# Picking the next expert tiles on GpSimd with one MAX8, and two small operations moved to GpSimd

## The chip, the cores and the metric

The kernel runs on one core of a Trainium2 chip. The metric is the time of one execution on the device in microseconds; the time shown is the median of three runs. Engines: TensorE (PE, with PEld for its weight loads), VectorE (DVE), ScalarE (ACT), GpSimd (POOL) and SyncE (SP), which here only issues DMAs.

## The reference

```python
# attention: q, k, v of 8 batches x 8 heads x 576 x 64
scores = scale * np.matmul(q, k.transpose(0, 1, 3, 2))
kth = np.partition(scores, -32, axis=-1)[..., -32:-31]
scores = np.where(scores >= kth, scores, -1e9)
attn = softmax(scores)                # exp, and the sum with 1e-9 added
x = np.matmul(attn, v)                # to 4608 rows of 512
# experts: 8, of 512 x 1024 x 512; each row goes to one
logits = x @ w_gate
e_idx = np.argmax(logits, axis=1)
gate_w = softmax(logits)[chosen]
eom = 1.0 / (1.0 + np.exp(-(x @ w_output_gate)))
out[mask] = gate_w * eom[:, e] * (np.maximum(x[mask] @ w1[e], 0.0) @ w2[e])
```

## The kernel before

**Attention steps.** The 4608 rows are 36 tiles of 128 queries. A step does two heads (an even and an odd one) of one tile, so a tile takes four steps and there are 144; four more rounds of the loop drain what is behind. In a step VectorE finds the largest of each group of scores (L305), ranks them (L312, L315) and, one step later, takes the largest of what lies below the 24th (L354) and chooses the 32nd (L365, `choose`). ScalarE copies the scores from PSUM (L286, called s), makes a sign against the 24th for each head (L339) and the exponentials (L349); GpSimd adds sign and scores (L342, two operations of 128x576) and copies two columns for a later check (L371, `near`). VectorE then multiplies the exponentials with the mask and sums them (`weigh`, L381). TensorE transposes the weights and multiplies with v.

**Lone heads.** In the first `LONE` steps the odd head isn't weighed on VectorE: `choose` writes the negated 32nd score to `LESS`, ScalarE makes a second sign with it (`veil`, L388), GpSimd adds sign and scores (L391), and two steps later ScalarE takes the exponential and the sum in one (`unveil`, L397). The steps that are below `LONE` are called calm: they have an order of their own, with the scores two steps ahead and with transposes of a constant that keep TensorE at work in every other step.

**Rows.** When a tile's four steps are through, `tile_rows` makes `r`, the reciprocal of the sums (an addition of 1e-9 and a reciprocal), computes its logits and writes its rows to memory. Tiles are in groups that end at the tiles listed in `SORTS`. After a group's last tile `group_route` finds the expert of each row, its place among the expert's rows and its weight, and `route` queues one scatter for each tile, which writes the row's index to that place.

**Slots.** A slot is up to 128 rows of one expert. After a group `slot_table` lists the next slots (`EARLY`: how many) from the counts of rows that wait; the last table, after all tiles, lists `USUAL` more, and code behind a condition handles any beyond these. A slot's steps are to load w1 and w2 (2 MB each) of its expert, load the list of rows (`fetch_id`), gather the rows (`fetch_x`), transpose them (`turn_ahead`) and do four pieces of products: two of `up` (L725) and two of `down` (L740). In the steps from `LONE` on, one piece is put into each step. After the last step the rest of the slots run in the tail, in another form: weights, rows and hidden values are split into a high and a low part (L1020, L1021), and three products of parts replace one (L1048).

**Queues.** Small VectorE work waits in `urgent` and `small`, and `fill(n)` issues n of it at fixed places of a step. A member of `small` that returns False stays ahead of the others. GpSimd's slow work (scatters, and the table in pieces of four operations) waits in `slow` with a cost and a due step; `run_slow` issues it up to a budget in each step. Engines work in the order of issue.

Of the kernel before, what the change touches and what calls it, by code (L numbers as in the profile page):

```python
# [33 lines left out]
DMAS = 2.0  # L34
# [5 lines left out]
def tile_topk_attention_moe(  # L40
# [50 lines left out]
    ENDS, EARLY, LEAST = zip(*sorts) if sorts else ((), (), ())  # L91
# [5 lines left out]
    for g in range(NGRP - 1):  # L97
        rest += len(GROUPS[g]) * P
        rest = min(rest, max(E * (LEAST[g] - 1), rest - EARLY[g] * LEAST[g]))
# [19 lines left out]
    first_row = consts.tile([1, E + 1], F32, name="first_row")  # L119
    slot_iota = consts.tile([1, MAXS, E], F32, name="slot_iota")  # L120
# [8 lines left out]
    def setup():  # L129
# [5 lines left out]
        def gates():  # L135
            for a in range(2):
# [12 lines left out]
               iota(first, [[-1, E]], E), iota(carry0, [[REG, E]]),  # L149
# [38 lines left out]
    def run(exact, stack):  # L188
# [170 lines left out]
        def choose(i):  # L359
# [3 lines left out]
            for a in range(2):  # L363
# [82 lines left out]
        done0 = consts.tile([1, E], F32, name="done0")  # L446
        nc.gpsimd.memset(done0, 0.0)
        DONE = [done0]
        rows_done = [0]

        def tile_rows(t, g, lg, j):
# [53 lines left out]
            urgent.append(lambda: nc.vector.tensor_scalar(r, sm, 1e-9, None, op0=ALU.add))  # L505
# [79 lines left out]
        def slot_table(g, last):  # L585

            n = NLAST if last else EARLY[g]
            least = 1 if last else LEAST[g]
            eng = nc.vector if last else nc.gpsimd
# [29 lines left out]
            add(lambda: eng.tensor_tensor(first_row[:, :E], first_row[:, :E], DONE[0], op=ALU.add))  # L619
            if last:  # L620
                def count():
                    NEED.append(consts.tile([1, 1], I32, name="need" + tagged))
                    eng.tensor_copy(NEED[0], T["d"][:, 7 + E:8 + E])
                    if not exact:
                        eng.tensor_scalar(over, T["d"][:, 7 + E:8 + E], -float(usual), 0.0, op0=ALU.add, op1=ALU.max)
# [630 lines left out]
```

## Time and profile before

| what | value |
|---|---|
| time, median of 3 runs | 1275.3 us (1271.2 to 1276.9) |
| the profiled execution's own time | 1271.3 us |
| its span, first to last instruction | 1269.5 us |
| mean granted TensorE clock | 0.99 |
| busy: TensorE, VectorE, ScalarE, GpSimd | 1178.2, 1196.9, 1043.9, 759.0 us |
| slots in all, by loads of w1 | 40 |

The busy times are sums over stages with different limits, so they don't say alone what sets the time. The time of an execution holds the span and what lies before the first and behind the last instruction.

### The profile page before, as it was taken

Reading aid. Unit: us, or ns where it says so; the run is one execution under the profiler, and the core shown is the slowest. Engines: PE = TensorE matmul, PEld = TensorE weight load, DVE = VectorE, ACT = ScalarE, POOL = GpSimd, SP = SyncE. Lnnn points to the kernel's source line nnn. Section 1 sums busy time; section 2 is a strip of 40 time slices with the busy share of each in tenths; the row PEclk is TensorE's granted clock in tenths of the full one; section 3 lists DMA queues with packets and bytes.
Section 4 is the critical chain, followed back from the end, with each engine's and each line's share of the span. In section 5 each row is a group of like instructions: output and inputs, shape, how many; then the busy total and the mean of one; then the engine's idle time right before and its main releaser. Section 6 shows DMA issues by size and latency. Waiting matters only on the chain.

```text
span 1269.5 us, 31280 instructions
## 1 busy us (share of the span) xinstructions
PE 1178.2 (93%) x9792; PEld 896.6 (71%) x9792; DVE 1196.9 (94%) x6157; ACT 1043.9 (82%) x1984; POOL 759.0 (60%) x1222
## 2 busy tenths in 40 slices
PE   6888778777699999999999999999999999999997
PEld 5665556555477777777777777777777777788885
DVE  7999999999999999999999999999999984898984
ACT  6999999898888878888888887888888763798884
POOL 6666666698775766757667667567657753132110
PEclk8999999999899999999999999999999999999999
DMA  5400210202818662765464555765554467999982
GB/s 138 77 18 19 71 55 18 56 19 64 290 57 278 202 225 104 249 229 159 174 205 159 211 189 164 258 221 177 207 179 162 151 202 248 373 399 386 379 311 82
DMA packets 109378, 227.41 MB, mean 179 GB/s; under 512 B 14858, under 2 KB 33546, under 8 KB 108176
## 3 DMA queue, kind: packets, MB, share of 16 engines
q1 hardware_dynamic: 99536, 205.67, 48.4%
q0 software_dynamic: 7552, 18.96, 4.3%
q8 instruction: 79, 1.29, 0.5%
q10 hardware_dynamic: 2112, 0.68, 0.3%
q14 instruction: 99, 0.81, 0.2%
HBM read 206.68 MB, written 20.69 MB: 179 GB/s over the span
## 4 chain that ended last, share of the span: by engine, by line
PE 59%; DVE 26%; issue 10%; DMA 2%; POOL 2%; ACT 1%; POOLq 0%; SPq 0%; ACTq 0%
PE pm L725 14%; PE pm L740 13%; PE po L440 10%; PE ps L278 9%; PE pst L408 9%; DVE cand L305 8%; DVE v L354 5%; DVE cand L315 3%; DVE v L312 3%; DVE ep L381 3%; DMA w1t<-in_w_dram 2%; DVE x L365 1%; PE pm L1048 1%; PE pst L461 1%; POOL xg L704 1%
## 5 line engine op out<-in xcount | busy, mean ns | idle before, releaser
L342 POOL TENSOR_TENSOR w<-s,marks 128x576 f32<-128x576 f32 x288 | 362.8, 1281 | 181.4 <-ACT marks L339 170.8
L305 DVE MAX8 cand<-s 128x8 f32<-128x72 f32 x2304 | 322.0, 218 | 8.1 <-ACT s L286 8.1
L408 PE MATMUL pst<-ident,ep 128*128 128x128 f32 x1296 | 206.8, 284 | 55.9 <-ACT ep L397 48.3
L339 ACT ACTIVATE marks<-s,v 128x576 int8<-128x576 f32 x288 | 220.9, 770 | 34.3 <-DVE v L312 30.8
L408 PEld LDWEIGHTS pst<-ident,ep 128*128 128x128 f32 x1296 | 145.8, 142 | 143.6 <-ACT ep L397 59.4
L416 ACT ACTIVATE pT<-pst 128x512 f32<-128x512 f32 (+1 forms) x432 | 197.7, 481 | 7.0 <-PE pst L408 5.2
L354 DVE MAX8 v<-w 128x8 f32<-128x576 f32 x288 | 202.1, 743 | 0.0
L286 ACT ACTIVATE s<-ps 128x1152 f32<-128x1152 f32 (+1 forms) x145 | 162.3, 1120 | 44.9 <-PE ps L278 44.9
L725 PE MATMUL pm<-xs,w1t 128*128 128x128 f32 x1664 | 194.7, 275 | 0.1
L725 PEld LDWEIGHTS pm<-xs,w1t 128*128 128x128 f32 x1664 | 189.9, 192 | 0.3 <-ACT y L747 0.3
L381 DVE SCALAR_TENSOR_TENSOR ep<-s,kth,ep 128x576 f32<-128x576 f32 x240 | 187.9, 812 | 0.3 <-issue 0.3
L278 PE MATMUL ps<-kst,qst 64*128 64x288 f32 (+1 forms) x1280 | 181.0, 431 | 5.4 <-ACT s L286 5.4
L440 PE MATMUL po<-pT,v 128*64 128x128 f32 (+3 forms) x3200 | 185.3, 267 | 0.0
L440 PEld LDWEIGHTS po<-pT,v 128*64 128x64 f32 (+1 forms) x3200 | 157.9, 136 | 33.0 <-issue 31.3
L740 PE MATMUL pm<-w2t,ht 128*128 128x512 f32 x400 | 180.5, 594 | 0.0
L349 ACT ACTIVATE ep<-s,v 128x576 f32<-128x576 f32 x240 | 175.5, 778 | 0.0
L751 POOL DMA_INDIRECT out_dram<-y,idt x40 | 46.6, 1165 | 181.4 <-ACT y L747 164.5
L312 DVE MAX8 v<-cand 128x8 f32<-128x64 f32 x864 | 148.2, 213 | 0.0
L278 PEld LDWEIGHTS ps<-kst,qst 64*128 64x128 f32 (+1 forms) x1280 | 97.7, 177 | 44.2 <-issue 16.1
L740 PEld LDWEIGHTS pm<-w2t,ht 128*128 128x128 f32 x400 | 72.1, 190 | 71.9 <-issue 71.9
L315 DVE MATCH_REPLACE8 cand<-v,cand 128x64 f32<-128x64 f32 x576 | 116.1, 209 | 0.0
L391 POOL TENSOR_TENSOR w<-s,marks 128x576 f32<-128x576 f32 x48 | 61.5, 1280 | 52.0 <-ACT marks L388 51.9
(183 smaller groups left out, 1837.6 us busy)
## 6 DMA issues: line engine op xcount, KB each, us to landing
w1t<-in_w_dram SPq DMA_DIRECT2D x40, 2048.0 KB, 10.0
w2t<-in_w_dram SPq DMA_DIRECT2D x40, 2048.0 KB, 11.9
v<-in_va_dram SPq DMA_DIRECT2D x8, 1152.0 KB, 5.7
x_rows<-xu SPq DMA_DIRECT2D x36, 256.0 KB, 2.6
qst<-in_qa_dram SPq DMA_DIRECT2D x70, 128.0 KB, 10.8
kst<-in_ka_dram SPq DMA_DIRECT2D x14, 576.0 KB, 7.8
ids<-far SPq DMA_DIRECT2D x1, 678.0 KB
xg<-x_rows,idt POOLq DMA_INDIRECT x40, 6.9
```

What stands on the lines that cost most here:

```text
L278: nc.tensor.matmul(ps[qs, a, n, :288], Q[t][rows, hp, qs], K[b][rows, hp, cols], start=True, stop=True)
L305: nc.vector.max(out=c[:, 8 * g:8 * g + 8], in_=SC[i, a][:, g * GW:(g + 1) * GW])
L312: nc.vector.max(out=vs[:, a, 8 * r:8 * r + 8], in_=cs[a])
L339: nc.scalar.activation(m.bitcast(I8).rearrange("p (s b) -> p s b", b=2)[:, :, 1], s, AF.Sign, bias=vs[:, a, PIVOT - 1:PIVOT], scale=-(1.0 ...
L342: nc.gpsimd.tensor_tensor(w, s, m, op=ALU.add)
L354: nc.vector.max(out=VV[i][0][:, a, 24:32], in_=SW[i][0][a])
L381: nc.vector.scalar_tensor_tensor(e, SC.pop((i, a)), kth_col(i, a), e, op0=ALU.is_ge, op1=ALU.mult, accum_out=SM[t][:, 2 * hp + a:2 * hp + ...
L408: nc.tensor.transpose(ps[:, c - c0, :], pt[:, c * P:(c + 1) * P], ident)
L416: nc.scalar.activation(x, ps[:, :n, :], AF.Copy)
L440: nc.tensor.matmul(po[a * 64:(a + 1) * 64, k, qs], lhs, rhs, start=half and not k and not m, stop=(c == 3 and k == 1 and m == len(TT[t]) - 1))
L725: nc.tensor.matmul(ph[:, f - f0, :], w[:, c, f * P:(f + 1) * P], XS[s][:, c, :], start=(c == 0), stop=(c == NC - 1))
L740: nc.tensor.matmul(PY[s], HT[s][:, f, :], w[:, f, :], start=(f == 0), stop=(f == NF - 1))
```

## The change

The plan `SORTS` has ten groups in place of nine, with 31 early slots in place of 29, and the last table lists 9 in place of 11. The first group, of four tiles, has no slots; the second ends at tile 7 as the first did before. `LONE` falls from 48 to 40. An early table is made by `slot_picks`: a key for each expert (the rows that wait, at most 128, with the expert's number to break ties), one MAX8 on VectorE that sorts the eight keys, and the first n of them; a slot no longer needs a least number of rows, and an expert gets at most one slot in a table. Its other operations run on GpSimd, or on VectorE for the first table. The negated 32nd score of a lone head and the addition of 1e-9 to the sums go from VectorE to GpSimd. The gather of a slot's rows may be issued one step after its list, not two; the budget of `run_slow` is 2.6 (2.0 in calm steps); the calls of `fill` take other numbers.

```diff
-SORTS = ((7, 3, 112), (10, 2, 96), (12, 3, 120), (15, 3, 80), (17, 4, 96), (20, 1, 128), (23, 4, 112), (27, 4, 128),
-         (31, 5, 64))
-
-USUAL = 11
+SORTS = ((4, 0), (7, 5), (11, 2), (13, 3), (16, 3), (19, 4), (23, 4), (27, 3), (30, 3), (32, 4))
+
+USUAL = 9
...
-DMAS = 2.0
+DMAS = 2.6
...
@@ -366,7 +368,7 @@
                                                op1=ALU.mult, accum_out=kth_col(i, a))
                 if lone(i, a):
                     LESS[i] = wk.tile([P, 1], F32, name="less", bufs=2)
-                    nc.vector.tensor_scalar(LESS[i], kth_col(i, a), -1.0, None, op0=ALU.mult)
+                    nc.gpsimd.tensor_scalar(LESS[i], kth_col(i, a), -1.0, None, op0=ALU.mult)
 
             nc.gpsimd.tensor_copy(NEAR[:, i], vs[:, :, PIVOT - 1:PIVOT + 2:2])
...
         CAR = [carry0]
-        done0 = consts.tile([1, E], F32, name="done0")
-        nc.gpsimd.memset(done0, 0.0)
-        DONE = [done0]
+        nc.gpsimd.iota(place[:, 1, :], pattern=[[REG, E]], base=0, channel_multiplier=0,
+                       allow_small_or_imprecise_dtypes=True)
...
             sm = SM.pop(t)
-            urgent.append(lambda: nc.vector.tensor_scalar(r, sm, 1e-9, None, op0=ALU.add))
+            nc.gpsimd.tensor_scalar(r, sm, 1e-9, None, op0=ALU.add)
             urgent.append(lambda: nc.vector.reciprocal(r, r))
             side.extend([gates, rows])
...
-        def slot_table(g, last):
-
-            n = NLAST if last else EARLY[g]
-            least = 1 if last else LEAST[g]
-            eng = nc.vector if last else nc.gpsimd
+        def slot_picks(g):
+
+            n = EARLY[g]
+
+            eng = nc.gpsimd if order else nc.vector
...
+            def key():
+                eng.tensor_tensor(tl("wait", [1, E]), CAR[0][0:1], place[:, 1, :], op=ALU.subtract)
+                eng.tensor_scalar(T["wait"], T["wait"], float(P), 2.0 * E, op0=ALU.min, op1=ALU.mult)
+
+                eng.tensor_tensor(tl("key", [1, E]), T["wait"], first[0:1], op=ALU.add)
+
+            def top():
+                nc.vector.max(out=tl("top", [1, E]), in_=T["key"])
+
+            def pick():
+                x = tl("pick", [1, E, E])[:, :n, :]
+                eng.tensor_tensor(x, T["key"][:, None, :].to_broadcast([1, n, E]),
+                                  T["top"][:, :n, None].to_broadcast([1, n, E]), op=ALU.subtract)
+                eng.tensor_scalar(x, x, 0.0, None, op0=ALU.is_equal)
+                tl("both", [1, 2, E, E])
+                for k in range(2):
+                    eng.tensor_tensor(T["both"][:, k, :n, :], x, place[:, k, None, :].to_broadcast([1, n, E]), op=ALU.mult)
+
+            def total():
+                x = T["both"][:, :, :n, :]
+                if eng is nc.vector:
+                    nc.vector.tensor_reduce(tl("slot", [1, 2, E])[:, :, :n], x, axis=AX.X, op=ALU.add)
+                    T["sum"] = T["slot"][:, :, :n]
+                else:
+                    for k in (4, 2, 1):
+                        eng.tensor_tensor(x[:, :, :, 0:k], x[:, :, :, 0:k], x[:, :, :, k:2 * k], op=ALU.add)
+                    T["sum"] = x[:, :, :, 0]
+
+            def slots():
+                SLOT[g] = st.tile([1, 2, E], I32, name="slots", bufs=3)
+                eng.tensor_copy(SLOT[g][:, :, :n], T["sum"])
+
+            def taken():
+                m = tl("taken", [1, E])
+                eng.tensor_tensor(m, T["key"], T["top"][:, n - 1:n].to_broadcast([1, E]), op=ALU.subtract)
+                eng.tensor_scalar(m, m, 0.0, 0.5 / E, op0=ALU.is_ge, op1=ALU.mult)
+                eng.tensor_tensor(m, m, T["wait"], op=ALU.mult)
+                eng.tensor_tensor(place[:, 1, :], place[:, 1, :], m, op=ALU.add)
+
+            if eng is nc.vector:
+                return [key, top, pick, total, slots, taken]
+            got = []
+
+            def part(cost, *fs):
+                def do():
+                    for f in fs:
+                        f()
+                    got.append(1)
+                return lambda: later("ids", cost, do, 3)
+            return [part(0.7, key), lambda: len(got) == 1, top, part(1.0, pick), part(0.8, total, slots), part(0.8, taken)]
...
-            add(lambda: eng.tensor_tensor(tl("cnt", [1, E]), CAR[0][0:1], carry0[0:1], op=ALU.subtract))
-            add(lambda: eng.tensor_tensor(tl("wait", [1, E]), T["cnt"], DONE[0], op=ALU.subtract))
+            add(lambda: eng.tensor_tensor(tl("done", [1, E]), place[:, 1, :], carry0[0:1], op=ALU.subtract))
+            add(lambda: eng.tensor_tensor(tl("wait", [1, E]), CAR[0][0:1], place[:, 1, :], op=ALU.subtract))
...
-            if not last:
-
-                add(lambda: eng.tensor_scalar(tl("t", [1, E + 1]), T["d"][:, 7:8 + E], -1.0, float(n),
-                                              op0=ALU.mult, op1=ALU.add))
...
-                add(dn)
...
-        LONE = 4 * ENDS[0] + 20 if ENDS else 0
+        LONE = 4 * min(t for t, n in sorts if n) + 12 if sorts else 0
...
-                ahead("turn", lambda s, *_: evs.append(turn(s, ps_t, "pst")), 1, "x", 2)
+                pool, name = (ps_t, "pst") if heavy else (ps_m, "pm")
+                ahead("turn", lambda s, *_: evs.append(turn(s, pool, name)), 1, "x", 2)
...
-                ops = slot_table(g, False)
-
-                def some(part):
-                    for f in part:
-                        f()
-                for x in range(0, len(ops), 4):
-                    part = ops[x:x + 4]
-                    small.append(lambda part=part: later("ids", 0.18 * len(part), lambda: some(part), 3))
+                small.extend(slot_picks(g))
...
-            ev = turn_ahead() if room else None
+            ev = turn_ahead() if room or not heavy else None
             if ev:
-                late.append(ev)
+                (last if calm else late).append(ev)
...
                 choose(i - 1)
-                fill(4 if calm else 1)
+                fill(5 if calm else 1)
                 weigh(i - 1)
-            ahead("x", fetch_x, 2, "id", 2)
-            run_slow(DMAS, ("ids", "out"))
+            ahead("x", fetch_x, 2, "id", 1)
+            run_slow(DMAS - 0.6 if calm else DMAS, ("ids", "out"))
...
-            fill(4 if calm else 3)
+            fill(3)
...
-        small_end = lambda: small.extend(slot_table(NGRP - 1, True) + [lambda: queue_slots(NGRP - 1, usual, N)])
+        small_end = lambda: small.extend(slot_table() + [lambda: queue_slots(NGRP - 1, usual, N)])
```

## Rows read from the trace of the kernel before

**Rows 1.** Windows: length, busy time of each engine, granted clock, DMA share, GB/s.
```profile
163.66:189.53 25.87, 20.78 (x197) 15.53 (x197) 25.66 (x162) 24.77 (x54) 17.59 (x23) 1.00 0.21 67
215.40:245.14 29.74, 22.79 (x205) 16.91 (x205) 29.40 (x177) 25.34 (x56) 17.75 (x25) 0.94 0.25 59
245.14:272.10 26.96, 21.57 (x206) 16.17 (x208) 26.75 (x165) 25.57 (x56) 22.97 (x36) 1.00 0.07 22
...
286.49:349.65 63.16, 45.36 (x418) 32.74 (x417) 62.46 (x376) 55.17 (x117) 51.60 (x87) 0.95 0.51 178
349.65:1009.80 660.15, 660.15 (x5806) 493.71 (x5806) 658.58 (x3760) 542.91 (x1105) 439.27 (x756) 1.00 0.57 190
```

**Rows 2.** Timeline of TensorE: start, length (us), engine, line, operation, tiles.
```profile
349.52 3.74 PE L725 MATMUL pm<-xs,w1t 128*128 128x128 f32 x32
...
1137.37 0.60 PE L1027 MATMUL pm<-ident,xg 128*128 128x128 f32 x4
...
1186.36 0.60 PE L1027 MATMUL pm<-ident,xg 128*128 128x128 f32 x4
```

**Rows 3.** Groups of instructions by line: count, busy us, mean ns, idle before.
```profile
L1020 ACT ACTIVATE w2h<-w2t 128x2048 fp32r<-128x2048 f32 x30 | 57.4, 1916 | 4.5 <-PE pm L1048 4.5
L704 POOL DMA_INDIRECT xg<-x_rows,idt x40 | 54.8, 1370 | 8.7 <-issue 6.3 <-PE ps L278 0.6 <-PE pm L1048 0.6
L505 DVE TENSOR_SCALAR r<-sums 128x8 f32<-128x8 f32 x36 | 6.1, 169 | 0.0
```

**Rows 4.** Timeline of one calm step, VectorE, ScalarE and GpSimd.
```profile
180.46 0.21 DVE L365 SCALAR_TENSOR_TENSOR x<-left,n,v 128x8 f32<-128x8 f32 x1
...
180.86 0.15 DVE L369 TENSOR_SCALAR less<-kth 128x1 f32<-128x1 f32 x1
...
181.11 0.78 ACT L388 ACTIVATE marks<-s,less 128x576 int8<-128x576 f32 x1
...
181.80 1.11 ACT L286 ACTIVATE s<-ps 128x1152 f32<-128x1152 f32 x1
...
182.81 0.59 ACT L416 ACTIVATE pT<-pst 128x512 f32<-128x512 f32 x1
...
183.29 0.78 ACT L339 ACTIVATE marks<-s,v 128x576 int8<-128x576 f32 x1
...
184.24 2.52 POOL L342 TENSOR_TENSOR w<-s,marks 128x576 f32<-128x576 f32 x2 [0.74 <-ACT marks L339]
...
186.70 0.19 POOL L371 COPY near<-v 128x4 f32<-128x4 f32 x1
186.72 0.21 DVE L365 SCALAR_TENSOR_TENSOR x<-left,n,v 128x8 f32<-128x8 f32 x1
```

**Rows 5.** Timeline of VectorE and of GpSimd where their operations overlap.
```profile
282.44 0.81 DVE L381 SCALAR_TENSOR_TENSOR ep<-s,kth,ep 128x576 f32<-128x576 f32 x1
...
282.51 0.83 POOL L628 TENSOR_SCALAR sl_jump<-sl_jump 1x8 f32<-1x8 f32 x1
...
361.99 0.24 POOL L628 TENSOR_SCALAR sl_jump<-sl_jump 1x8 f32<-1x8 f32 x1
...
1006.04 0.82 DVE L365 SCALAR_TENSOR_TENSOR x<-left,n,v 128x8 f32<-128x8 f32 x1
...
1006.78 0.19 POOL L371 COPY near<-v 128x4 f32<-128x4 f32 x1
...
1006.97 0.82 DVE L381 SCALAR_TENSOR_TENSOR ep<-s,kth,ep 128x576 f32<-128x576 f32 x1
```

**Rows 6.** Timeline of VectorE after the last tile: route of five tiles, last table.
```profile
1062.07 0.20 DVE L524 TENSOR_REDUCE mx<-lg 128x5 f32<-128x40 f32 x1
...
1065.24 0.15 DVE L602 TENSOR_TENSOR sl_cnt<-base,carry 1x8 f32<-1x8 f32 x1
...
1069.84 0.18 DVE L646 CAST slots<-sl_slot 1x46 int32<-1x46 f32 x1
```

**Rows 7.** DMA issues: operation, count, KB of each, median us to landing.
```profile
xg<-x_rows,idt POOLq DMA_INDIRECT x40, 6.9
```

More of the change, by code (lines that the diff above doesn't have):

```diff
@@ L90, in tile_topk_attention_moe @@
     sorts = [x for x in SORTS if x[0] < NTT]
-    ENDS, EARLY, LEAST = zip(*sorts) if sorts else ((), (), ())
+    ENDS, EARLY = zip(*sorts) if sorts else ((), ())
+    assert all(n <= E for n in EARLY) and E == 8
     ends = list(ENDS) + [NTT]
@@ L119, in tile_topk_attention_moe @@
     first_row = consts.tile([1, E + 1], F32, name="first_row")
+    place = consts.tile([1, 2, E], F32, name="place")
     slot_iota = consts.tile([1, MAXS, E], F32, name="slot_iota")
@@ L590, in slot_table @@
+        def slot_table():
+            n = NLAST
+            least = 1
+            eng = nc.vector
             ops = []
@@ L618, in slot_table, with count @@
             add(lambda: eng.tensor_scalar(first_row[:, :E], T["d"][:, 7:7 + E], -float(P), None, op0=ALU.mult))
[L619 to L625, printed above, removed]
-                add(count)
+            add(lambda: eng.tensor_tensor(first_row[:, :E], first_row[:, :E], T["done"], op=ALU.add))
+            def count():
+                NEED.append(consts.tile([1, 1], I32, name="need" + tagged))
+                eng.tensor_copy(NEED[0], T["d"][:, 7 + E:8 + E])
+                if not exact:
+                    eng.tensor_scalar(over, T["d"][:, 7 + E:8 + E], -float(usual), 0.0, op0=ALU.add, op1=ALU.max)
+            add(count)
             add(lambda: eng.tensor_tensor(tl("jump", [1, E]), first_row[:, 1:], first_row[:, :E], op=ALU.subtract))
@@ L643, in slots @@
             def slots():
-                SLOT[g] = (consts.tile([1, 2, MAXS], I32, name="slots" + tagged) if last else
-                           st.tile([1, 2, MAXS], I32, name="slots", bufs=3))
-                eng.tensor_copy(SLOT[g][:, :, :n], T["slot"][:, :, :n])
+                SLOT[NGRP - 1] = consts.tile([1, 2, MAXS], I32, name="slots" + tagged)
+                eng.tensor_copy(SLOT[NGRP - 1][:, :, :n], T["slot"][:, :, :n])
             add(slots)
-            if not last:
-                add(lambda: eng.tensor_scalar(tl("t", [1, E + 1]), T["d"][:, 7:8 + E], -1.0, float(n),
-                                              op0=ALU.mult, op1=ALU.add))
-                add(lambda: eng.tensor_scalar(T["t"], T["t"], 0.0, None, op0=ALU.max))
-                add(lambda: eng.tensor_tensor(T["t"][:, :E], T["t"][:, :E], T["t"][:, 1:], op=ALU.subtract))
-                add(lambda: eng.tensor_scalar(T["t"][:, :E], T["t"][:, :E], float(P), None, op0=ALU.mult))
-                add(lambda: eng.tensor_tensor(T["t"][:, :E], T["t"][:, :E], T["wait"], op=ALU.subtract))
-                add(lambda: eng.tensor_scalar(T["t"][:, :E], T["t"][:, :E], 0.0, None, op0=ALU.min))
-                def dn():
-                    d = st.tile([1, E], F32, name="done", bufs=2)
-                    eng.tensor_tensor(d, T["cnt"], T["t"][:, :E], op=ALU.add)
-                    DONE[0] = d
-                add(dn)
             return ops
```

8 lines of the change are left out of this document (6 added, 2 removed).

## The prediction

> **What bounds the kernel now.** I cut the span into stages first, because the share of busy time means something else in each [rows 1]. GpSimd's operation of L328 runs once in a step, so its starts mark the 144 steps. In the calm steps a tile of four steps takes 25.87 us, with VectorE busy for 25.66 and ScalarE for 24.77: two engines near their limit. From step 51, when the first expert slot starts [rows 2], to step 140, 89 steps take 660.15 us, 7.42 each; TensorE is busy for all of it, VectorE for 658.58. In the last stretch only experts are left. I then read the timeline of the tail: the transposes of a slot's rows come 49.0 us apart over four slots, 12.25 each [rows 2]. The split of w2 has 30 entries, two a slot, so 15 of the 40 slots run there and 25 in the plain form among the attention steps [rows 3]. Last I read one calm step and the places where a VectorE and a GpSimd instruction overlap [rows 4, 5].
>
> **The change part by part.**
> Slots. The plan before is 29 early and 11 late; after, 31 and 9: 40 either way, if nine hold what is left. From the reference's inputs (seed 0) I counted the tokens that each expert has waiting after ten rounds of picks and the last four tiles: 108, 75, 106, 73, 130, 123, 45 and 126, which fill 1+1+1+1+2+1+1+1 = 9 slots. They just fit.
>
> The start. Slot n of the plain form starts at step s+4n. Before, s is 51, so slot 24 starts at 147, the last round of the loop, and three of its four pieces run behind it. With s = 42 slot 26 starts at 146 and two pieces run behind. Written out, the new order of the work gives 41 to 43: the group that makes the first table has three tiles, not seven, so three scatters, and with nothing queued yet its 14 small operations run on VectorE at once instead of a few a step on GpSimd; the gather goes one step after the ids, not two. I take 42. So 27 slots run in the plain form and 13 in the tail: **-24.5 us** (two at 12.25 [rows 2]). One plain piece less behind the loop is **-3.7** [rows 2]. Nine steps turn from light into heavy: steps 42 to 50 took 63.16 us, 7.02 each, heavy ones take 7.42 [rows 1], so 9 x 0.40 = **+3.6**. The two uncalm steps without a slot move from 48, 49 to 40, 41; I allow **+0.6**.
>
> Supply. The groups that end at tiles 11 to 30 leave 16 steps from their last tile to the step that needs their first slot; my count of the queue's rounds comes to 13 to 15 with the gather and the turn. No gap is priced, one is a rival.
>
> The odd head's negated 32nd score on GpSimd. On VectorE it takes 0.15 us [rows 4], which brings the weighting of the even head (L381) forward by that, 0.6 a tile. But ScalarE's second sign (L388) waits for this number. In the trace a GpSimd operation that reads on-chip memory and starts while L381 runs does not end before it: one began 0.07 us into L381, took 0.83 instead of 0.24, and ended 0.09 behind it [rows 5]; 69 of the 81 small operations that start around an L381 look like this one, nine of the others start up to 0.02 before it and three only write. L381 follows the last instruction of the choice (L365) at once, before GpSimd can see its result. So the number comes behind L381. What is late next: L388, then in ScalarE's order the copy of the scores, a copy of pT and the next step's first sign (L339), then GpSimd's two additions (L342). These end level with VectorE's arrival at L365 today (186.70 against 186.72 [rows 4]). And L365 is held while an addition runs: one took 0.82 instead of 0.21 and ended 0.08 after GpSimd had begun its next operation, L371 [rows 5]. So the delay closes a loop. From the end of one pair, which L371's start marks, to the end of the next: 0.19 from L371's start to L381, 0.82 for it, 0.09, 0.10 to ScalarE, 2.18 from L388 to L339, 0.95 to the additions, 2.46 for them: 6.79 us a step [rows 4, 5], a tile 27.2 instead of 25.87, +1.3. Bound below: if the wait costs nothing, the relief of 0.6 a tile is left. Above: L388 comes 1.20 behind the pair instead of 0.65 behind L365's start, 0.55 on each of some 30 steps, +17. I take the loop: 6.5 undisturbed calm tiles give +8.4.
>
> The Trainium skill has a rule that speaks against this part ("SBUF — State Buffer", section "Who interferes with whom"): a VectorE instruction with two operands in SBUF and a GpSimd instruction that reads SBUF exclude each other, and whichever was issued first keeps the other out to its end. The trace agrees with it in both directions (0.83 for 0.24, 0.82 for 0.21). Applied here it gives -10.4 us for the whole change; if it did not bite in these steps, -23.9.
>
> Routes. One more group is routed (tiles 0 to 3): its 16 operations took 3.2 us on VectorE for the last group, 0.5 of it a wait [rows 6]. Steps that VectorE paces hide the loop, so this tile comes to 25.87 + 2.7 - 0.6, **+2.1**. The tile that routed seven tiles took 29.74; it routes three now, some 28.0, **-1.7** [rows 1]. The next took 26.96 with GpSimd's table; now it is three steps of the loop and one with the first table on VectorE (14 operations at 0.18, from 27 in 4.8 us [rows 6]), some 29.0, **+2.0**. Calm steps together 8.4 + 2.1 - 1.7 + 2.0 = **+10.8**.
>
> The other eight tables lose 17 of 32 GpSimd operations each, which nothing on the path waits for: TensorE paces these steps. But VectorE's MAX8 is put behind GpSimd's three operations for its key, and VectorE's next ranking and choice queue behind it. The key is issued as VectorE enters its two L381; each holds an operation back, so the key ends some 0.5 us behind VectorE's step, later with a gather (1.4 [rows 3]) ahead. VectorE has slack there, the held L365s. I take 0.3 a table, **+2.4**; bounds 0 and, with a gather and three held operations at 0.8 in full, 3.8 each.
>
> The addition to the sums: 36 times 0.17 us leaves VectorE [rows 3], where TensorE's heavy steps and the loop hide it; without that cover it would be 6.1. The reciprocal behind it comes a step later, when GpSimd has mostly passed; a wait like the loop's 0.09 + 0.10 each time would be 7. I take nothing. The last table works on a longer list (34 rows for 23): **+0.4**, from 4.8 us for the whole [rows 6]. The other DMA budgets and the order of a turn's copy issue the same work: nothing.
>
> Sum: -24.5 - 3.7 + 3.6 + 0.6 + 10.8 + 2.4 + 0.4 = **-10.4 us**. The profiled execution took 1271.3 us (a span of 1269.5 and 1.8 around it), so 1260.9. The median shown is 4.0 above it; I put 1262, a little towards it. A measurement of this kernel can tell about 0.5%, 6.4 us.
>
> **The rivals.**
> *The late number is harmless.* ScalarE is idle for 1.1 us of a calm tile [rows 1], which might take up the wait. Then the calm terms are -3.9 + 2.1 - 1.7 + 0.8 = -2.7 for +10.8, total -23.9, 1247. Against it: L388 to L339 shows ScalarE without a gap [rows 4].
> *The slots don't come.* If the first slot is four steps late, or a gap of four arises, one slot goes back to the tail: +12.25 less 4 x 0.40, 1271.5: the change wouldn't do what it says. For it: my count leaves one to three steps.
> *VectorE waits for GpSimd's key (slower).* Place: the MAX8 in the eight tables of the heavy steps. With a gather and three held operations ahead it waits 3.8 us, 30 in all for the 2.4: 1289. From 2.5 us a table the sum is over 6.4 above the time before. Against it: VectorE's two L381 run meanwhile, and held L365s are slack.
> *Nine slots don't hold the rest.* The guarded extra slots run one behind the other, each at least 12.25 and the landing of its rows, 6.9 [rows 2, 7]: one adds 19, 1280, two 1299. It decides from a tenth slot; the count says nine, with experts at 123 and 126 of 128.
>
> **How the numbers follow.** The loop in the calm steps with the tail's gain, 0.52; harmless 0.25; slots late 0.10; key 0.07; tenth slot 0.02; the rest 0.04. The likeliest case has its own range, 1255 to 1269 (the loop's term 5 to 15, the start 41 to 43). The 8-in-10 range goes to the harmless case below and a little above no change: 1246 to 1277. Faster by over 0.5%: the harmless case, three quarters of the likeliest (0.39) and half the rest, 0.66. Within: most of the remaining likeliest (0.12) and the late slots, 0.22. Slower: the key, the tenth slot and what is left of the others, 0.12.
>
> **What would show it.** Step starts by L328: calm tiles of 27.2 where they took 25.9. The negated score on GpSimd lasting some 0.8 us and ending 0.1 behind L381, with ScalarE's L388 waiting for it, and L365 lasting up to 0.9 in calm steps. The first L725 at step 42; 26 entries in w2's split; a tail two slots shorter at 12.25 each. Heavy steps at 7.42 and VectorE's waits for GpSimd under 3 us in all. The prediction is wrong if calm tiles stay at or under 25.9 (then 1247), if heavy tiles grow, or if the tail keeps 14 or 15 slots.

## The result: slower, and the profile after

The changed kernel takes 1280.1 us (median of 8 runs, 1278.8 to 1281.6), the kernel before 1273.8 on the same chip: a ratio of 1.0054, with a 95% interval of 1.0045 to 1.0064. I had forecast 1262, with 1246 to 1277 as the range: wrong in direction, and outside the range. The profiled execution took 1280.9 us, a span of 1279.1 for the 1269.5 of before: +9.6 where my sum said -10.4.

In the attention steps the line numbers of the changed kernel are 2 higher: L367 is the choice, L383 the weighting, L341 and L390 ScalarE's signs, L344 GpSimd's additions, L371 the negated score.

The windows of the changed kernel come first: a calm tile, the two tiles at the first table and the first slot, steps 44 to 50, steps 51 to 139, and a stretch behind the loop (columns as in [rows 1]).

```profile
171.25:198.01 26.76, 19.82 (x194) 15.16 (x190) 26.73 (x156) 23.79 (x52) 24.08 (x34) 1.00 0.21 65
253.02:286.26 33.24, 25.29 (x211) 19.79 (x208) 32.93 (x179) 24.76 (x53) 24.66 (x33) 0.79 0.27 65
286.26:318.77 32.51, 27.66 (x219) 21.50 (x221) 29.15 (x151) 25.45 (x55) 17.03 (x23) 0.95 1.04 370
318.77:371.33 52.56, 52.56 (x468) 40.55 (x464) 52.42 (x299) 43.05 (x88) 27.97 (x41) 1.00 0.50 173
371.33:1042.29 670.96, 664.80 (x5819) 493.45 (x5813) 648.24 (x3751) 542.06 (x1105) 404.79 (x665) 1.00 0.56 188
1092.10:1105.07 12.97, 3.83 (x18) 1.70 (x16) 10.64 (x53) 2.73 (x5) 8.13 (x14) 0.74 0.73 268
```

The calm tile stands at 26.76 us for 25.87 [rows 1]. The tile with the first table (the second row) takes 33.24 for the 26.96 that this tile took before; the next one 32.51 for 27.12. Steps 51 to 139 take 670.96 for 660.15, and TensorE, busy for all of them before, is now idle for 6.2 us of them. In the last row it is busy for 3.83 of 12.97. By stages, beside the forecast:

| stage | measured, us | forecast, us |
|---|---|---|
| steps 0 to 35 | +7.9 | +8.8 |
| steps 36 to 39 (first table) | +6.3 | +2.0 |
| steps 40 to 50 | +7.5 | +4.2 |
| steps 51 to 139 | +10.8 | +2.4 |
| step 140 to the tail's first plain piece | -0.3 | -3.7 |
| from there to the end | -22.6 | -24.1 |
| sum | +9.6 | -10.4 |

Three more views of the changed kernel. One calm step on VectorE, GpSimd and ScalarE, to be read beside [rows 4]:

```profile
186.88 1.08 DVE L367 SCALAR_TENSOR_TENSOR x<-left,n,v 128x8 f32<-128x8 f32 x1
...
188.08 0.82 DVE L383 SCALAR_TENSOR_TENSOR ep<-s,kth,ep 128x576 f32<-128x576 f32 x1
...
188.21 0.77 POOL L371 TENSOR_SCALAR less<-kth 128x1 f32<-128x1 f32 x1 [0.28 <-DVE x L367]
188.93 0.18 POOL L373 COPY near<-v 128x4 f32<-128x4 f32 x1
...
189.01 0.78 ACT L390 ACTIVATE marks<-s,less 128x576 int8<-128x576 f32 x1 [0.85 <-POOL less L371]
```

The negated score (L371) starts 0.13 us into L383, lasts 0.77 and ends 0.08 behind it; ScalarE's second sign (L390) waits 0.85 for it, and the choice (L367) is held for 1.08. This is the loop as predicted, at a smaller price: this tile takes 26.76 us where 27.2 was forecast. Next the groups (count, busy us, mean ns, idle before them):

```profile
L1061 ACT ACTIVATE w2h<-w2t 128x2048 fp32r<-128x2048 f32 x26 | 49.7, 1916 | 4.0 <-PE pm L1089 4.0
L390 ACT ACTIVATE marks<-s,less 128x576 int8<-128x576 f32 x40 | 31.2, 779 | 21.5 <-POOL less L371 21.4
L506 POOL TENSOR_SCALAR r<-sums 128x8 f32<-128x8 f32 x36 | 9.2, 256 | 2.7
L604 DVE MAX8 sl_top<-sl_key 1x8 f32<-1x8 f32 x9 | 1.4, 157 | 11.8 <-POOL sl_key L601 11.5
L798 POOL DMA_INDIRECT out_dram<-y,idt x40 | 44.9, 1123 | 199.1 <-ACT y L794 186.5 <-issue 12.6
```

The split of w2 has 26 entries, so 13 slots are left for the tail, as forecast. New are VectorE's 11.5 us before the MAX8 (L604). And GpSimd's idle time before the scatter of a slot's result (L798): most of the 186.5 lies in the tail, where it harms nobody, but in steps 51 to 139 the waits of the two kernels (us in total, times, longest) are these; first after:

```profile
POOL out_dram L798 <- ACT y L794: 51.8, 22, 3.0
DVE sl_top L604 <- POOL sl_key L601: 11.5, 5, 2.5
DVE r L507 <- POOL r L506: 9.7, 5, 2.2
```

and before (the same instruction is L751 there):

```profile
POOL out_dram L751 <- ACT y L747: 14.3, 8, 2.4
```

Last, TensorE at the end of the loop in the changed kernel (L183 is TensorE's part of the flag, the check that the columns copied by `near` are for):

```profile
1092.10 3.60 PE L787 MATMUL pm<-w2t,ht 128*128 128x512 f32 x8
...
1104.95 0.19 PE L183 MATMUL po<-lo,ones 128*1 128x2 f32 x2 [9.14 <-DVE gap L178]
1105.07 5.53 PE L772 MATMUL pm<-xs,w1t 128*128 128x128 f32 x32
```

Between the last plain piece and the tail's first one TensorE waits 9.14 us for the flag (L174 to L188), which stands on VectorE behind the last route and the last table. In the kernel before, with three plain pieces there, it waited 1.00:

```profile
1072.78 0.19 PE L181 MATMUL po<-lo,ones 128*1 128x2 f32 x2 [1.00 <-DVE lo L179]
```

### The profile page after: what moved, and what is told of

Same layout as the page of the kernel before. It is cut to its first block, busy times and chain, and to the rows that moved or that the text cites. A ratio compares the mean times of both kernels' runs of the same rounds, so it can differ in the third digit from the quotient of the medians.

```text
span 1279.1 us, 31046 instructions
## 1 busy us (share of the span) xinstructions
PE 1174.6 (92%) x9769; PEld 895.5 (70%) x9769; DVE 1184.7 (93%) x6113; ACT 1018.9 (80%) x1958; POOL 728.5 (57%) x1124
## 4 chain that ended last, share of the span: by engine, by line
PE 59%; DVE 23%; issue 10%; POOL 5%; ACT 2%; DMA 1%; POOLq 0%; SPq 0%; ACTq 0%
PE pm L772 14%; PE pm L787 14%; PE po L442 10%; PE ps L280 8%; PE pst L410 8%; DVE cand L307 7%; DVE v L356 4%; DVE cand L317 3%; DVE v L314 3%; DVE x L367 2%; DVE ep L383 2%; PE pm L1089 1%; PE pst L462 1%; POOL w L344 1%; DMA w1t<-in_w_dram 1%
## 5 line engine op out<-in xcount | busy, mean ns | idle before, releaser
L344 POOL TENSOR_TENSOR w<-s,marks 128x576 f32<-128x576 f32 x288 | 362.8, 1281 | 176.4 <-ACT marks L341 176.4
L341 ACT ACTIVATE marks<-s,v 128x576 int8<-128x576 f32 x288 | 220.7, 771 | 54.8 <-DVE v L314 50.9
L410 PE MATMUL pst<-ident,ep 128*128 128x128 f32 x1296 | 203.0, 283 | 51.5 <-ACT ep L399 37.9
L772 PE MATMUL pm<-xs,w1t 128*128 128x128 f32 x1792 | 213.3, 278 | 0.0
L772 PEld LDWEIGHTS pm<-xs,w1t 128*128 128x128 f32 x1792 | 207.8, 194 | 0.2 <-issue 0.2
L383 DVE SCALAR_TENSOR_TENSOR ep<-s,kth,ep 128x576 f32<-128x576 f32 x248 | 194.8, 816 | 0.3 <-issue 0.3
L787 PE MATMUL pm<-w2t,ht 128*128 128x512 f32 x432 | 194.4, 593 | 0.0
L351 ACT ACTIVATE ep<-s,v 128x576 f32<-128x576 f32 x248 | 181.0, 779 | 0.0
L798 POOL DMA_INDIRECT out_dram<-y,idt x40 | 44.9, 1123 | 199.1 <-ACT y L794 186.5
L787 PEld LDWEIGHTS pm<-w2t,ht 128*128 128x128 f32 x432 | 77.9, 190 | 77.7 <-issue 77.5
L367 DVE SCALAR_TENSOR_TENSOR x<-left,n,v 128x8 f32<-128x8 f32 x288 | 86.3, 335 | 0.0
```

The lines of the kernel that those rows point to most:

```text
L341: nc.scalar.activation(m.bitcast(I8).rearrange("p (s b) -> p s b", b=2)[:, :, 1], s, AF.Sign, bias=vs[:, a, PIVOT - 1:PIVOT], scale=-(1.0 ...
L344: nc.gpsimd.tensor_tensor(w, s, m, op=ALU.add)
L383: nc.vector.scalar_tensor_tensor(e, SC.pop((i, a)), kth_col(i, a), e, op0=ALU.is_ge, op1=ALU.mult, accum_out=SM[t][:, 2 * hp + a:2 * hp + ...
L410: nc.tensor.transpose(ps[:, c - c0, :], pt[:, c * P:(c + 1) * P], ident)
L772: nc.tensor.matmul(ph[:, f - f0, :], w[:, c, f * P:(f + 1) * P], XS[s][:, c, :], start=(c == 0), stop=(c == NC - 1))
L787: nc.tensor.matmul(PY[s], HT[s][:, f, :], w[:, f, :], start=(f == 0), stop=(f == NF - 1))
```

## The experiments

Each time below is the median of its runs, and each ratio is to the kernel before, measured beside it on the same chip; the changed kernel stands at 1.0054, and "less" or "more" without another name is against it. A run that adds lines to the kernel shifts the line numbers behind them.

### The score back on VectorE

```diff
-                    nc.gpsimd.tensor_scalar(LESS[i], kth_col(i, a), -1.0, None, op0=ALU.mult)
+                    nc.vector.tensor_scalar(LESS[i], kth_col(i, a), -1.0, None, op0=ALU.mult)
```

> The changed kernel with one part undone: the odd head's negated 32nd score is worked out on VectorE again, behind the choice, as in the kernel before. Theory: in the calm steps this number comes behind the weighting on GpSimd (mean 684 ns), ScalarE's second sign waits for it, and the calm tiles take 26.6 to 26.8 us for 25.9. Undone, the tiles fall back to 25.9 to 26.0, step 36 starts 6 to 9 us earlier, and the time falls from 1280 to 1271 to 1274, ratio to the changed kernel 0.993 to 0.995. Rival: the calm tiles grew because of the other edits of these steps (more small operations for each step, the turn's copy at the end, the transfers' budget): then step 36 moves by under 1 us and the time stays at 1279 to 1281.

1273.1 us, ratio 1.0005 (0.9996 to 1.0014): 0.49% less, 6.2 us. A calm tile in the windows of this run:

```profile
191.65:217.31 25.66, 20.50 (x197) 15.54 (x197) 25.49 (x160) 24.74 (x54) 17.91 (x24) 1.00 0.08 22
```

The theory holds: the calm tiles fall from 26.8 to 25.7, and step 36 starts 6.4 us sooner.

### The score alone, in the kernel before

The same line of the kernel before (L369), on GpSimd.

> The kernel before with one edit of the change alone: the odd head's negated 32nd score on GpSimd. Theory: the loop of GpSimd's late number, ScalarE's second sign and GpSimd's additions lengthens each calm tile by 0.7 to 1.3 us there too: over its 48 calm steps 7 to 11 us, a ratio of 1.005 to 1.009. Rival: the loop closes only with the changed kernel's order of the calm steps (one more small operation ahead of the weighting): within 2 us of the kernel before.

1282.0 us, ratio 1.0082 (1.0068 to 1.0096): 10.4 us more than the kernel before, by itself more than the whole change lost. The total lies in the range of the theory, but its parts do not. An undisturbed calm tile rises by some 0.5 us (25.87 to 26.41 here), less than the 0.7 to 1.3 of the theory:

```profile
195.00:221.41 26.41, 20.27 (x199) 15.62 (x197) 26.34 (x157) 24.57 (x54) 20.69 (x26) 1.00 0.07 21
```

The three tiles of steps 36 to 47 rise by 2.0 to 2.6 us each (29.48 for 26.96 in the first), 7.1 us of the 10.8 that the trace is behind at step 48. In them GpSimd also issues scatters and gathers and makes its first table; which of these makes the late number dearer there no run separates. The group of ScalarE's second sign there:

```profile
L388 ACT ACTIVATE marks<-s,less 128x576 int8<-128x576 f32 x48 | 37.5, 782 | 26.6 <-POOL less L369 26.3
```

### The addition to the sums back on VectorE

```diff
-            nc.gpsimd.tensor_scalar(r, sm, 1e-9, None, op0=ALU.add)
+            nc.vector.tensor_scalar(r, sm, 1e-9, None, op0=ALU.add)
```

> The changed kernel with the addition to the sums back on VectorE, at the same place in the order, so that nothing else moves. Theory: the reciprocal behind it waits on VectorE for GpSimd (16.6 us over 36 times, 9.7 of it in the heavy steps and 6.9 at the last tile), and part of this lengthens the steps behind a group's end: without it the waits for GpSimd on that line vanish and the time falls by 2 to 6 us, to 1274 to 1278. Rival: TensorE paces these steps and the waits are slack, so that the time changes by less than 1 us, or grows by up to 3 us as 36 additions of 0.17 us go back to VectorE.

1279.0 us, ratio 1.0051 (1.0039 to 1.0064): no change that the intervals can tell. The theory falls. The waits for this number are gone, and part of what its removal from VectorE had given went with them: in the trace the tile of steps 72 to 75 (a group has just ended) falls from 32.94 to 30.82, and the next one rises from 28.13 to 29.52. In all, this trace has steps 51 to 139 at 666.56 us, 4.4 shorter, but is 1.5 behind at step 51, and the times show no gain.

### The flag behind four pieces of the tail

```diff
-        if not settled and small_end is None and not small:
-            unsettled(st, ps_o)
-            settled = True
-        for _ in slots_in_turn():
+        for n, _ in enumerate(slots_in_turn()):
             background()
+            if n == 3 and not settled and small_end is None and not small:
+                unsettled(st, ps_o)
+                settled = True
```

> The changed kernel with the flag of the tail (six operations on 128x288 numbers and the product that TensorE adds up) put behind the first four pieces of the tail instead of ahead of them; the same work. Theory: with one plain piece behind the loop instead of three, VectorE's chain of route, last table and flag is uncovered and TensorE stands idle for 9.1 us before the tail's first plain piece. With the flag later, that piece starts at once (some 9 us earlier), and the slot behind it starts when its weights have landed and are split, some 4 to 6 us earlier: the time falls by 3 to 6 us, to 1274 to 1277. Rival: the tail is paced by VectorE's splits, which stand behind the table either way, and the flag's 3.5 us only move to a later place on VectorE: the time changes by less than 1 us.

1278.5 us, ratio 1.0050 (1.0037 to 1.0063): a miss, because of the place that I chose. The first piece starts 9 us sooner, but the flag's product then stands in TensorE's order ahead of the next slot's transposes, while VectorE is still busy with splits:

```profile
1096.24 3.82 PE L772 MATMUL pm<-xs,w1t 128*128 128x128 f32 x32
...
1120.23 0.19 PE L183 MATMUL po<-lo,ones 128*1 128x2 f32 x2 [3.37 <-DVE lo L181]
```

### The flag behind all slots

```diff
-        if not settled and small_end is None and not small:
-            unsettled(st, ps_o)
-            settled = True
         for _ in slots_in_turn():
```

> The changed kernel with the flag of the tail behind all slots instead of ahead of the first; the same work. The placement behind four pieces made TensorE wait 3.4 us for it there, which took back much of what was gained. Theory of the seam: the tail's first slot starts some 9 us earlier, the next 6 us earlier, the steady slots follow at 12.25 us each, and the flag at the end hides behind the landing of the last rows: the time falls by 3 to 6 us. Rival: the steady slots can't start earlier, as the stream of weights (a share of 0.95 to 1.04 of the DMA engines from the seam on) sets their pace: the time stays within 1 us, and the idle time turns up between the first two slots.

1276.9 us, ratio 1.0029 (1.0019 to 1.0040): 0.25% less, 3.2 us. TensorE at the end of the loop:

```profile
1091.01 3.60 PE L787 MATMUL pm<-w2t,ht 128*128 128x512 f32 x8
1094.57 3.82 PE L772 MATMUL pm<-xs,w1t 128*128 128x128 f32 x32
...
1106.09 0.49 PE L1089 MATMUL pm<-w1h,xsh 128*128 128x512 f32 x1 [3.69 <-ACT xsh L1061]
```

The idle time behind the loop was worth 3.2 of its 9.1 us: for the rest, what follows the two pieces waits for its weights, as the rival has it. ScalarE, which splits them, shows that wait:

```profile
1103.16 1.91 ACT L1061 ACTIVATE w1h<-w1t 128x2048 fp32r<-128x2048 f32 x1 [7.83 <-DMA w1t<-in_w_dram]
```

### The MAX8 one step later

```diff
-                    got.append(1)
+                    got.append(step[0])
...
-            return [part(0.7, key), lambda: len(got) == 1, top, ...
+            return [part(0.7, key), lambda: len(got) == 1 and step[0] > got[0], top, ...
```

> The changed kernel in which VectorE's MAX8 of a slot table is issued one step later, so that GpSimd's key is there when VectorE comes to it; the same work, the slots' places one step later. Theory: VectorE's 11.5 us of waits for the key in five tables push the ranking and the choice behind them, and the tiles behind a group's end are long (31 to 33 us for 28 to 30) for that reason: the waits on that line fall under 2 us, and the time falls by 2 to 7 us, to 1273 to 1278. Rival: these tiles are long because TensorE and ScalarE have the routing products and copies there, and VectorE's wait only takes the place of another: under 1 us of change, or up to 2 us more where a slot's supply comes late.

1293.1 us, ratio 1.0165 (1.0152 to 1.0178): 14 us more. Between steps 51 and 139 VectorE waits 4.0 us for the key instead of 11.5, and the tile of steps 72 to 75 is 1.2 us shorter. But one group's slots came too late: the tile of steps 56 to 59 took 44.1 us for 28.0. The waits there:

```profile
DVE r L507 <- POOL r L506: 16.5, 2, 13.8
...
POOL xg L751 <- DMA idt<-ids: 13.8, 1, 13.8
PE pst L544 <- POOL oh L538: 13.7, 1, 13.7
```

A gather (L751) stood on GpSimd 13.8 us for its list of rows, and with it the sums' addition, which VectorE waits for, and a zero fill, which TensorE waits for. The supply, which I had counted as one to three steps ahead, has no step to give in this group.

### The scatter one step later

```diff
             for x in [x for x in slow if x[2] in kinds]:
+                if x[2] == "out" and x[0] > step[0]:
+                    continue
                 if spent[0] + x[3] > budget:
```

> The changed kernel in which GpSimd issues the scatter of a slot's result one step after the slot's last product, never in the same step; the same work, and every slot starts in the same step. Theory: with the transfers' budget at 2.6 the scatter is issued in the step of its slot's last product, GpSimd stands for ScalarE's copy of that product (57.8 us in 24 scatters of the heavy steps, 14.3 in 8 before), and the table's key and the addition to the sums stand behind it on GpSimd, so that VectorE waits 11.5 and 9.7 us for them. With the scatter a step later these three waits fall below 20, 4 and 4 us, and the time falls by 4 to 10 us, to 1270 to 1276 where the kernel before takes 1273. Rival: the key is late because of VectorE's weighting, which holds GpSimd's small operations back, and because of the gather: the waits of VectorE stay near 20 us, and the time changes by under 1 us.

1273.9 us, ratio 1.0001 (0.9991 to 1.0011): 0.53% less, 6.7 us. What the scatter did in the changed kernel, on GpSimd and then on VectorE:

```profile
442.30 0.09 POOL L797 MEMSET spacer<- 1x1 f32 x1
445.09 1.06 POOL L798 DMA_INDIRECT out_dram<-y,idt  x1 [2.70 <-ACT y L794]
446.18 0.20 POOL L598 TENSOR_TENSOR sl_wait<-base,place 1x8 f32<-1x8 f32 x1
446.46 0.27 POOL L599 TENSOR_SCALAR sl_wait<-sl_wait 1x8 f32<-1x8 f32 x1
446.81 0.19 POOL L601 TENSOR_TENSOR sl_key<-sl_wait,first 1x8 f32<-1x8 f32 x1
...
447.04 0.16 DVE L604 MAX8 sl_top<-sl_key 1x8 f32<-1x8 f32 x1 [2.37 <-POOL sl_key L601]
```

The scatter is issued in the step of its slot's last product and waits 2.70 us for ScalarE's copy of it; the key, whose inputs are there, stands behind it for 3.8 us, and VectorE behind the key for 2.37. In the run with the scatter a step later the list of waits of steps 51 to 139 has no MAX8 and no `y` any more; of waits for GpSimd it names

```profile
DVE r L509 <- POOL r L508: 9.7, 5, 2.2
...
ACT marks L343 <- POOL v L332: 0.2, 1, 0.2
```

and these steps take 663.40 us, with TensorE busy for 663.04 again. The wait of the reciprocal is still there at 9.7; a later run, with the addition on VectorE, shows that it costs nothing. My theory was wrong on this one of the three waits. Whether the key's wait alone carried the 6.7 us no run separates.

The Trainium skill ("Perfetto Trace Analysis", section "Tensor Engine Instruction (MATMUL, LD_WEIGHTS)") says that the execution queues of VectorE, ScalarE and GpSimd are strictly first in, first out; the key, held for 3.8 us behind the scatter, agrees.

### The budget alone, in the kernel before

```diff
-            run_slow(DMAS, ("ids", "out"))
+            run_slow(2.6 if heavy else DMAS, ("ids", "out"))
```

> The kernel before with the transfers' budget at 2.6 instead of 2.0 once slots run; every slot starts in the same step. Theory: the higher budget alone lets GpSimd issue a scatter in the step of its slot's last product, behind a gather: GpSimd's waits for ScalarE's copy of the product rise from 14.3 us toward 50, and the kernel gets longer by 1 to 5 us, though its GpSimd tables are waited for by nobody. Rival: what puts the scatter into that step in the changed kernel is the start of its slots one step nearer to the even steps that attend: the waits stay under 25 us and the time within 1 us.

1275.8 us, ratio 1.0036 (1.0023 to 1.0050): 4.6 us more than the kernel before. The scatter's waits in steps 51 to 139, and the window of these steps:

```profile
POOL out_dram L751 <- ACT y L747: 34.4, 17, 2.6
351.44:1010.73 659.29, 659.24 (x5791) 492.80 (x5792) 657.73 (x3751) 542.03 (x1104) 429.73 (x763) 1.00 0.56 187
```

A gather and a scatter are reckoned at 1.1 each. Their 2.2 are above a budget of 2.0, so that before, the scatter went to the next step; they are below 2.6. So the constant by itself brings back the waits, 17 for 8. But the theory of their price is not borne out. The steps take 659.29 us for the 660.15 of before, with TensorE busy for all but 0.05 of it, and no VectorE operation in them waits for GpSimd. Of the 4.2 us by which the span of this trace is longer, 1.8 stand at step 51, ahead of which the edit does nothing; the distance is the same 1.8 where the tail begins (1074.75 for 1072.90), and the rest comes behind that. Where the 4.6 us come from stays open. The changed kernel with a budget of 2.0 was not run.

### The score and the scatter together, with and without the sums' addition

> The changed kernel with the negated score on VectorE again and the scatter one step later, two parts at once; the table and the addition to the sums stay on GpSimd. Theory: the two causes lie in different steps, so they add up: 6 to 7 us from the calm steps and 4 to 10 from the heavy ones, 1263 to 1270 where the kernel before takes 1273, a ratio to it of 0.992 to 0.998, faster than both kernels. Rival (the heavy steps grew for another reason): the ratio stays at 1.000.

> As the run with the score and the scatter, and the addition to the sums on VectorE too. Theory: VectorE paces the heavy steps, since without GpSimd's addition the tiles that end a group got shorter by 10 us in sum and the others longer by 7. Once GpSimd comes in time, the addition on GpSimd is a gain: this kernel is slower than the one with the addition on GpSimd by 2 to 6 us. Rival: TensorE paces them, and the two come out within 1 us.

With the score and the scatter put right 1265.3 us, ratio 0.9935 (0.9921 to 0.9948): the two add up. With the addition on VectorE as well 1265.1 us, the same ratio: the rival is right, and this addition is worth nothing in either place.

### All three parts, and then the first table

The first of these runs adds the flag's place, with the three diffs shown.

> The changed kernel with three parts put right: the negated score on VectorE, the scatter one step later, the flag of the tail behind all slots. Theory: the three gains (6.2, 6.8 and 3.2 us, each by itself) lie in different stretches and add up; the kernel with the first two stands at a ratio of 0.9935 to the kernel before, so this one comes to 0.990 to 0.992. Rival: the flag's gain hangs on what came ahead of it, and the ratio stays at 0.993 to 0.994.

The second makes the first table on GpSimd too:

```diff
-            eng = nc.gpsimd if order else nc.vector
+            eng = nc.gpsimd
```

> As the run with the three parts put right, and the first table on GpSimd like the others; the first slot then starts some two steps later, and three plain pieces run behind the loop. Theory: the tile that makes the first table took 31.2 us where 29 had been reckoned, because VectorE's 14 operations are held one by one while GpSimd adds; on GpSimd the tile falls to 28 to 29, and as the two pieces fit into TensorE's idle time behind the loop, the whole falls by 1 to 3 us more, a ratio of 0.988 to 0.990. Rival: the tile is long because of its route and its gathers: no change, or 1 to 3 us longer where supply comes late.

The three parts: 1261.4 us, ratio 0.9918 (0.9905 to 0.9932). With the first table on GpSimd 1252.1 us, ratio 0.9845 (0.9832 to 0.9859): far more than the theory's 1 to 3 us, and 20 us faster than the kernel before (1272.3 beside it). The two tiles at the first table and the first slot, first with three parts:

```profile
247.33:279.24 31.91, 24.35 (x208) 18.99 (x204) 31.46 (x181) 25.03 (x53) 22.68 (x30) 0.84 0.28 61
279.24:311.82 32.58, 27.71 (x219) 21.56 (x221) 29.20 (x153) 25.41 (x55) 16.27 (x23) 0.95 1.05 352
```

and with the first table on GpSimd:

```profile
246.07:272.01 25.94, 21.53 (x217) 16.43 (x216) 25.77 (x161) 24.21 (x54) 24.33 (x43) 0.99 0.06 14
272.01:298.95 26.94, 21.57 (x173) 15.94 (x175) 26.87 (x153) 24.13 (x52) 18.48 (x25) 0.87 1.04 379
```

Inside the first tile with three parts, a table operation on VectorE, GpSimd's addition beside it, and ScalarE's sign in the next step:

```profile
253.60 1.26 DVE L629 CAST slots<-sl_slot 1x10 int32<-1x10 f32 x1
253.56 1.27 POOL L395 TENSOR_TENSOR w<-s,marks 128x576 f32<-128x576 f32 x1 [0.21 <-ACT marks L392]
...
258.37 0.78 ACT L343 ACTIVATE marks<-s,v 128x576 int8<-128x576 f32 x1 [3.19 <-DVE v L316]
```

The lower clock is not what makes this tile long: with the score and the scatter put right alone, and in the next run, it takes 31.19 us at a granted clock of 0.95.

### The table's place and the slots' start, apart

The first run is the one with three parts, with the first slot held back to step 43 and the table on VectorE; the second is the changed kernel with the table's line alone, which also starts the first slot at step 43.

```diff
-            if heavy or when.get(("turn", s), clock[0]) >= clock[0]:
+            if heavy or step[0] < 43 or when.get(("turn", s), clock[0]) >= clock[0]:
```

> As the run with the three parts put right, the first table still on VectorE, but the first slot held back to step 43, where the run with the first table on GpSimd had it. Theory: the table's place and the start each have their own price: the tile that makes the table stays at 31 to 32 us (25.9 on GpSimd), and only the next tile, which loses the two heavy steps 41 and 42, falls from 32.6 to 27 or 28; the rest of the way grows by 2 to 3, so that the kernel gains 2 to 4 us, a ratio of 0.988 to 0.990. Rival: the start is the whole cause (the early rows and weights disturb the tile that makes the table): the tile falls to 26 to 28 and the ratio to 0.984 to 0.986. Second rival: the table's place is the whole cause: the ratio stays at 0.992.

> The changed kernel with one edit alone: the first table is made on GpSimd like the other eight, and the first slot starts two steps later. Theory: of the changed kernel's loss, the tile of the first table and the one behind it (33.2 and 32.5 us) are the largest single part; they fall to 27 to 28 each, some 9 us come back in all, to a ratio of 0.996 to 0.999. Rival: the gain hangs on the scatter and the score that were put right beside it: under 4 us, 1.002 or more.

Held back: 1258.8 us, ratio 0.9885 (0.9868 to 0.9903). The table alone: 1272.0 us, ratio 0.9985 (0.9976 to 0.9994), 0.69% or 8.8 us less than the changed kernel. In it the two tiles take 28.96 and 27.36 us for 33.24 and 32.51, with the late score still in them. The same two tiles with the start held back:

```profile
246.53:277.72 31.19, 22.28 (x208) 16.44 (x204) 30.74 (x181) 24.93 (x53) 22.47 (x29) 0.95 0.27 64
277.72:305.14 27.42, 21.67 (x187) 15.96 (x189) 27.35 (x153) 24.76 (x53) 15.77 (x22) 0.94 1.05 375
```

So both have a price, as the theory said: the tile that makes the table stays at 31.2 and falls to 25.9 only with the table on GpSimd; the next falls by 5.2 as it loses two pieces. In the run of the table alone the flag's wait behind the loop fell too, since three plain pieces run there again:

```profile
1095.60 0.19 PE L183 MATMUL po<-lo,ones 128*1 128x2 f32 x2 [1.24 <-DVE lo L181]
```

## Why the prediction was wrong

**What held.** The late score was the term that I argued most, and it came out: the stage of the calm steps +7.9 for +8.8, with the order of events as told (0.77 us for a short operation, held by L383, L367 held in turn). That the sum came so close is in part luck: six of the calm tiles rose by 0.7 to 0.9 us and not by 1.3, while that of steps 4 to 7 rose by 1.8 and step 0 began 0.5 later. The rule of the Trainium skill ("SBUF — State Buffer", section "Who interferes with whom"), that a VectorE instruction with two operands in SBUF and a GpSimd instruction that reads SBUF shut each other out, was borne out in the calm step shown (the score's 0.77 us, ending 0.08 behind L383). Nine late slots held the rest, 26 entries are in w2's split, the steady tail runs at 12.25 us a slot, and the sums' addition is worth nothing. The first slot came at step 41, inside the 41 to 43 that I gave, not at the 42 that I summed with.

**The step that failed first: "The other DMA budgets ... issue the same work: nothing."** The work is the same; its step is not. In the changed kernel the scatter is issued in the step of its own product, and GpSimd stands for ScalarE. That this costs 6.7 us is shown by moving the scatter. That the constant of 2.6 brings it there is shown in the kernel before, where it raises these waits from 14.3 to 34.4 us; there these steps get no longer, so the price lies in what VectorE waits for behind the scatter, which only the changed kernel has; this last is argued and not shown. The term for the MAX8, +2.4, named the right wait and the wrong cause: I reckoned with VectorE's weighting and a gather ahead of the key; it was the scatter, and without it the trace shows no wait for the key. What is left of steps 51 to 139 is 663.40 for 660.15, +3.2; why is open.

**Second: the first table on VectorE, "some 29.0", and 0.40 a heavy step.** The tile took 33.24. I had put 14 operations at 0.18 on one of its four steps. Of it 2.0 us are the late score's (31.19 with the score back on VectorE). In the run with three parts the second half of the table stands as one block of 3.0 us between a step's choice and its weighting, one operation in it is held to 1.26 us and one ahead of it to 1.98, each to the end of an addition on GpSimd, and ScalarE's sign then waits 3.2 us for VectorE's ranking. The table's place is worth 0.40%, 5 us (the ratios of the two runs that start at step 43, 0.9885 and 0.9845). The first two pieces, at steps 41 and 42, cost 5.2 us in their tile and not 0.8: the mean of later heavy steps was the wrong row for the first ones. Why they cost so much is settled in part only. TensorE had waited 3.9 us for ScalarE ahead of the first piece, which then took 5.23 us at a granted clock of 0.70; with the start held back it took 3.74 at 1.00.

```profile
296.55:301.78 5.23, 5.23 (x35) 5.23 (x35) 5.23 (x24) 1.77 (x4) 3.51 (x5) 0.70 1.05 387
```

**Third: -3.7 for a plain piece less behind the loop.** Those pieces covered the chain of route, last table and flag on VectorE (12.4 us here, 11.7 before). With the start at step 41 one piece is left of three, two pieces less and not one; the cover was gone, and the stage gave 0.3 us, where two pieces would be 7.4 by my term. This is the question that I asked of other edits and not of this one: what does the removed work hide? The flag's place gives 3.2 back.

The terms of the three failed steps miss by 4.3 + 3.3 + 8.4 + 3.4 = 19.4 of the 20.0 us between -10.4 and +9.6. Every rival that I gave put the loss into a thing that the change does on purpose; it came from a constant, a place and an end that the diff touches by the way.

## What to carry to other kernels

On an engine that runs its queue in order, a budget or a due time is an edit of the order: for each transfer that may now be issued earlier, look whether its data is there at that step, and who waits for what stands behind it. A small operation moved to another engine costs what its reader waits, not its own time, and one held operation in a loop is paid each time round (0.15 us moved in each calm step, 6 to 10 us lost). When work is taken away from a place where two engines meet, ask what it covered, and price the first steps of a new phase from a row of a first step.

## What the runs showed of the hardware

One table operation on 1x8 numbers (the key of the first table) took 1.98 us on VectorE, for 0.15 to 0.2 otherwise, and ended 0.02 behind GpSimd's addition; so the holding also hits the smallest operations. It had begun 0.67 ahead of that addition, while GpSimd issued a scatter; what held it until then no row settles. Behind the 9.1 us in which TensorE waited, its first 32 products took 5.53 us at a granted clock of 0.68 in the mean, that is partly at 1.2 GHz and partly at 2.4; without the idle time before them (the flag behind all slots) the same products took 3.82 at 1.00. The windows of these products, first of the changed kernel:

```profile
1105.07:1110.60 5.53, 5.53 (x36) 5.53 (x35) 2.87 (x5) 0.69 (x1) 0.59 (x2) 0.68 0.99 290
```

and with the flag behind all slots:

```profile
1094.57:1098.39 3.82, 3.82 (x40) 3.82 (x37) 3.30 (x21) 0.69 (x1) 2.38 (x5) 1.00 0.83 287
```
